# Local and strided attention into a gated mixture of four attentions: wider value products and a fixed order of TensorE's work

## The chip, the cores and the metric

The kernel runs on one core of a Trainium2 chip, in one launch. The metric is the device time of that launch in microseconds. The core has a matrix engine (TensorE, PE in the rows; its weight loads are shown as an engine of their own, PEld), a vector engine (DVE), a scalar engine (ACT), GpSimd (POOL) and SyncE (SP), which issues the transfers here. All five work at once and wait for each other through semaphores. TensorE writes into PSUM, which has eight banks of 128 x 512 floats; the other engines copy from there to SBUF.

## The reference, cut to what matters

```python
# first part: 8 batches, 8 heads, 576 positions, 64 columns a head
rel = pos[:, None] - pos[None, :]
mask_local = (rel >= 0) & (rel < 32)
mask_strided = (rel >= 0) & (pos[None, :] % 32 == pos[:, None] % 32)
# heads 0 to 3 use mask_local, heads 4 to 7 mask_strided
attn = softmax(where(mask, q @ k.T / 8, -1e9))
x = attn @ v                          # heads side by side: 576 x 512 for a batch
# second part: 4 experts, each an attention of 64 columns over x; a token uses its best 2
logits = x @ w_gate
for e in range(4):
    a = softmax(causal(x @ wq[e] @ (x @ wk[e]).T / 8))
    out += weight_of_e_in_the_top_2 * (a @ (x @ wv[e]) @ wo[e])
```

## The kernel before, in words

A batch goes through two stages. **stage1** takes a pair of heads (four pairs a batch: two local, two strided). It loads q and k (`load_qk`, SP), transposes them on TensorE (`tp`, line 875), computes the scores (`s`, line 908), masks them (DVE), runs a softmax in six steps on DVE, POOL and ACT (lines 932 to 943), brings the probabilities the other way round (`tr` on DVE for local heads, `pt` on TensorE at line 972 for strided ones), multiplies with v (`xa`, line 1000 local, line 1019 strided) and splits the result into two numbers of fewer bits, `xh` and `xl`. **The second stage** works on a batch of x: projections (`pj`, lines 1125 and 1136; `vp`, line 1072), scores (`s2`, line 1210; `s2_4`, line 1190), a softmax whose last step is a scaling on POOL (`scale2`, line 1245), transposes (`t2`, line 1264), the product with the values (`acc`, line 1297) and the output matrix (`yp`, line 1326).

A local head looks at 32 positions back, so its 576 queries are 18 blocks of 32, and a block needs the keys of two blocks: the one before and its own. Blocks 0 to 4 stand in partitions 0 to 31, blocks 5 to 9 in the next 32, and so on (`c`, four groups). The product with v at line 1000 takes for every block and each of the two heads two matmuls: 32 partitions, the 64 columns of v as weights, 32 columns of probabilities. These are 35 x 2 = 70 matmuls for a pair of heads, and an f32 matmul runs as two pairs of a weight load and a matmul, so 140 pairs.

TensorE's array is used in **six shapes of tile**, called modes in the code: 128x128 (`pj`, `vp`, `s2_4`, `yp`), 64x128 (`tp`, `pt`, `t2`, `s2`), 128x64 (`acc`), 64x64 (strided `s` and `xa`), 64x32 (local `s`) and 32x64 (local `xa`).

No engine's order is written out by hand. `op(kind, engines, key, function, ...)` records an operation with a modelled duration, and `schedule()` then emits all of them engine by engine: whenever an engine is free in its model it takes, of the operations that could start first, the one with the smallest key. The key is a due time plus a number from a table `PRI` (one row for each kind and batch). For TensorE five is added to the key if the mode would change:

```python
k = o.key + (MODE_PEN if e == "PE" and mode not in (None, o.mode) else 0.0)
...
if t < 26.0:
    d *= 1.5
if mode not in (None, o.mode):
    d += 0.09 + o.first
elif t > free[e] + 0.05:
    d += 0.08
```

On the chip every engine then works through its list in that order and waits in place for what is not ready. What schedule() chooses also decides which of the eight banks (`RB`), which of two buffers of probabilities (`P2`) and which of two input buffers (`NAT`) an operation gets.

Of the kernel before, what the change touches and what calls it, by code (L numbers as in the profile page):

```python
# [14 lines left out]
NEG = -1.0e9  # L15
# [5 lines left out]
def attention_moe_kernel(  # L21
# [26 lines left out]
    STR = 32  # L48
# [15 lines left out]
    class Op:  # L64
        __slots__ = ("eng", "key", "fn", "mode", "npk", "allocs", "uses", "succ", "ndep", "ready", "end", "left", "first")
# [15 lines left out]
    class Ring:  # L81
# [16 lines left out]
        def take(self, buf):  # L98
# [1305 lines left out]
```

## Time and profile before

| what | value |
|---|---|
| median of 3 runs | 522.42 us (514.83 to 523.39) |
| the profiled execution | 523.32 us, its span 521.6 us |
| PE busy | 478.3 us, 92% of the span, 9,126 weight loads and as many matmuls |
| DVE, ACT, POOL busy | 328.4, 288.7 and 201.9 us |
| moved by the DMA queues | 42.05 MB, 81 GB/s over the span |
| mean granted clock of TensorE | 0.930 of full speed |

The table is read from the top: the engine with the largest busy share first, then what share the others have. Busy time of PE is not time at full rate: a matmul of few columns holds the engine for its passage while others run beside it in other tiles, so the prediction measures from start to start.

### The profile page before, as it was taken

To read this page: it belongs to the slowest core of one execution; us is meant where nothing else is said; L and a number is where in the kernel's file an instruction comes from. 1 tells how busy PE (TensorE), PEld (TensorE's weight loads), DVE (VectorE), ACT (ScalarE), POOL (GpSimd) and SP (SyncE) were. 2 spreads that over 40 slices of the span, in tenths; PEclk is the share of its full clock that TensorE was granted. 3 is DMA by queue.
4 is the path that set the end of the run, shared out by engine and by line. 5 is a ranking of instruction groups with operands and counts; after the bars stand their busy time and mean duration, and the time that the engine had idled before them with its cause. 6 is when DMAs were issued, how large, how long until landed. Compare 5 with 4: busy or idle time off the path is not lost.

```text
span 521.6 us, 21771 instructions
## 1 busy us (share of the span) xinstructions
PE 478.3 (92%) x9126; PEld 422.0 (81%) x9126; DVE 328.4 (63%) x1057; ACT 288.7 (55%) x870; POOL 201.9 (39%) x320
## 2 busy tenths in 40 slices
PE   6668989998897999998898999979999799999996
PEld 5557879996676799997777899769987798789874
DVE  4745947567865665776677546768787346863850
ACT  3335647655865434666585435754487226762862
POOL 5443725434722241456145212733265013720440
PEclk9555999999989899999889999989999799999999
DMA  7566571207436432301334620274013400210013
GB/s 144 125 146 139 116 129 35 53 1 136 132 88 143 112 81 55 88 2 30 72 98 120 167 88 1 71 142 106 7 48 110 124 1 25 63 64 0 1 63 101
DMA packets 83777, 42.05 MB, mean 81 GB/s; under 512 B 71904, under 2 KB 75360, under 8 KB 83680
## 3 DMA queue, kind: packets, MB, share of 16 engines
q1 hardware_dynamic: 83680, 40.67, 32.3%
q8 instruction: 72, 1.18, 1.0%
q14 instruction: 25, 0.20, 0.1%
HBM read 31.20 MB, written 9.44 MB: 78 GB/s over the span
## 4 chain that ended last, share of the span: by engine, by line
PE 83%; DMA 6%; issue 5%; SPq 3%; DVE 2%; ACT 0%; ACTq 0%; DVEq 0%
PE bank L1125 17%; PE bank L1072 11%; PE bank L1326 11%; PE bank L1297 9%; PE bank L1210 6%; DMA nat<-in_k_dram 6%; PE bank L1264 5%; PE bank L1000 5%; PE bank L875 4%; PE bank L908 4%; PE bank L1190 3%; PE bank L1136 3%; PE bank L1019 3%; PE bank L972 2%; SPq L822 2%
## 5 line engine op out<-in xcount | busy, mean ns | idle before, releaser
L1245 POOL TENSOR_SCALAR p<-p,st,wt 128x512 f32<-128x512 f32 (+3 forms) x128 | 76.5, 613 | 66.6 <-DVE st L1229 25.5
L1222 ACT ACTIVATE p<-p,st 128x128 f32<-128x128 f32 (+3 forms) x128 | 71.5, 562 | 10.2 <-DVE st L1217 10.1
L1217 DVE CUSTOM_DVE_ANT_0 p<-bank,m_cau 128x256 f32<-128x256 f32 (+3 forms) x128 | 55.6, 486 | 5.1 <-PE bank L1210 4.6
L683 ACT COPY th<-bank 128x384 f32<-128x384 f32 (+2 forms) x117 | 45.7, 434 | 13.8 <-PE bank L1264 12.7
L683 ACT COPY qkt<-bank 128x324 f32<-128x324 f32 (+2 forms) x99 | 36.8, 426 | 29.1 <-PE bank L875 24.8
L1297 PE MATMUL bank<-th,vs 128*64 128x192 f32 (+4 forms) x512 | 52.5, 355 | 0.0
L1145 ACT CAST qk<-bank 128x288 fp32r<-128x288 f32 x64 | 25.5, 398 | 48.2 <-PE bank L1125 43.4
L934 POOL TENSOR_TENSOR p1l<-p1l,st 128x640 f32<-128x640 f32 (+1 forms) x18 | 20.5, 1141 | 73.3 <-DVE st L932 55.5
L986 DVE TENSOR_TENSOR xl<-bank,xh 128x160 fp32r<-128x160 f32 (+4 forms) x112 | 31.3, 327 | 26.8 <-ACT xh L984 26.1
L1297 PEld LDWEIGHTS bank<-th,vs 128*64 128x64 f32 x512 | 35.5, 143 | 14.8 <-issue 8.1
L984 ACT CAST xh<-bank 128x160 fp32r<-128x160 f32 (+4 forms) x112 | 27.3, 322 | 36.4 <-PE bank L1000 30.9
L1147 DVE TENSOR_TENSOR qkl<-bank,qk 128x288 fp32r<-128x288 f32 x64 | 28.7, 452 | 29.0 <-ACT qk L1145 28.7
L875 PE MATMUL bank<-ident,nat 54*128 54x54 f32 (+1 forms) x636 | 35.3, 252 | 12.4 <-DMA nat<-in_k_dram 7.8
L1072 PE MATMUL bank<-wh_v,xh 128*128 128x260 f32 (+1 forms) x160 | 46.2, 289 | 0.1
L1072 PE MATMUL bank<-wl_v,xh 128*128 128x260 f32 (+1 forms) x160 | 46.0, 288 | 0.3 <-DVE wl_v L778 0.3
L1072 PE MATMUL bank<-wh_v,xl 128*128 128x260 f32 (+1 forms) x160 | 46.1, 288 | 0.0
L1000 PE MATMUL bank<-pt,v 32*64 32x32 f32 x2240 | 30.5, 232 | 15.6 <-issue 15.3
L1000 PEld LDWEIGHTS bank<-pt,v 32*64 32x64 f32 x2240 | 27.8, 140 | 18.9 <-issue 17.2
L875 PEld LDWEIGHTS bank<-ident,nat 54*128 54x128 f32 (+1 forms) x636 | 29.5, 162 | 16.6 <-issue 6.5
L1264 PE MATMUL bank<-ident,p 64*128 64x64 f32 x800 | 41.2, 231 | 0.2
L1264 PEld LDWEIGHTS bank<-ident,p 64*128 64x128 f32 x800 | 33.1, 141 | 8.3 <-issue 4.8
L908 PE MATMUL bank<-qkt 64*32 64x64 f32 (+1 forms) x2048 | 35.2, 245 | 2.7 <-issue 1.9
(146 smaller groups left out, 1320.6 us busy)
## 6 DMA issues: line engine op xcount, KB each, us to landing
out_dram<-ys SPq DMA_DIRECT2D x32, 256.0 KB
nat<-in_k_dram SPq DMA_DIRECT2D x28, 144.0 KB
nat<-in_q_dram SPq DMA_DIRECT2D x28, 144.0 KB
nat<-in_q_dram SPq DMA_DIRECT2D x32, 99.0 KB
nat<-in_k_dram SPq DMA_DIRECT2D x32, 99.0 KB
v<-in_v_dram SPq DMA_DIRECT2D x64, 48.0 KB
v<-in_v_dram SPq DMA_DIRECT2D x48, 54.0 KB
nat<-in_q_dram SPq DMA_DIRECT2D x16, 90.0 KB
```

Of the source, the lines that this page charges most:

```text
L683: (nc.scalar.copy if e == "ACT" else nc.vector.tensor_copy)(dst, src)
L875: nc.tensor.transpose(tp[x].t[:, w_ * (g - g0):w_ * (g - g0) + w_], blk, ident[r, r])
L908: nc.tensor.matmul(o, lhs, rhs, start=True, stop=True)
L1000: nc.tensor.matmul(xa[c].t[64 * h:64 * h + 64, 32 * i:32 * i + 32], vv()[r, h, i + own, :], pv2()[r, h, i, 32 * own * (g > 0):32 * own * ( ...
L1072: nc.tensor.matmul(vp.t[:m, :NV], xx.t[:, t0:t0 + m], ww.t[:, kt, :], start=i == 0, stop=i == 11)
L1125: nc.tensor.matmul(pj.t[:, :HS], ww.t[:, kt, ep * 128:(ep + 1) * 128], xx.t[:, c], start=i == 0, stop=i == 11)
L1217: lambda e, sp=sp, p=p, a=a, nk=nk, ci=ci: nc.vector.tensor_tensor_reduce(out=p.t[:, a, :nk], in0=sp[a].t[:, :nk], in1=m_cau[:, S - nk:], ...
L1222: op("exp2", {"ACT": 0.33 + 0.00083 * nk}, k_ + 1, lambda e, p=p, a=a, ci=ci, nk=nk: nc.scalar.activation(p.t[:, a, :nk], p.t[:, a, :nk], ...
L1245: lambda e, p=p, a=a, ci=ci, t=t, nk=nk: nc.gpsimd.tensor_scalar(p.t[:, a, :nk], p.t[:, a, :nk], st.t[:, 14 + ci + a:15 + ci + a], wt.t[:, ...
L1264: nc.tensor.transpose(tp[hf].t[:, 64 * c:64 * c + 64], src, ident[r, r])
L1297: nc.tensor.matmul(acc.t[o, c0:c0 + cn], vw, th[a].t[:, s0:s0 + cn], start=j == 0, stop=j == idx[-1], skip_group_check=True)
L1326: nc.tensor.matmul(yp.t[:, :DM], xx.t[:, c0:c0 + 128], ww.t[:, ep, :], start=i == 0, stop=i == 5)
```

## The change

Three things change, and the table of numbers.

First, at line 1000 (1014 after) a matmul no longer serves one query block. A block of v is the "own" block of one query block and the "block before" of the next, and both stand side by side in the transposed probabilities. So one matmul with 64 columns of probabilities writes both; at the ends of a group of five it has 32. A pair of heads has 21 x 2 = 42 matmuls, 84 pairs. To make that regular, query block 0 has keys before the start of the sequence as its first 32 columns, and the mask sets them to -1e9 with one memset in place of a memset and a POOL selection.

Second, on TensorE `PRI` no longer holds numbers that are added to a due time but the places of the operations in one sequence, 0, 1, 2 and so on; `schedule()` takes them in that order, and waits in its model if the next one is not ready. `MODE_PEN` goes. The other engines keep keys, with new numbers.

Third, the model counts TensorE's instructions (`ni` pairs an operation): they come in parts of 256, a part is asked for 40 instructions before the part ahead of it begins, and it is there 4.0 us later; TensorE waits at its first instruction until then. This is in the model alone; nothing on the chip is changed by it but the order that follows.

```diff
-        o.eng, o.fn, o.mode, o.npk = eng, fn, mode, npk
+        o.eng, o.fn, o.mode, o.npk, o.ni = eng, fn, mode, npk, 2 * ni
...
-        o.key = round(key + PRI[at][SEQ[at]], 3)
+        o.key = PRI[at][SEQ[at]] if "PE" in eng else round(key + PRI[at][SEQ[at]], 3)
...
+    FETCH = 4.0
...
+        turn = 0
+        done, ask, part, here, coming = 0, 193 - 40, 193, 0.0, 0.0
...
+                if e == "PE":
+                    cand = [o for o in cand if o.key == turn]
...
-                        k = o.key + (MODE_PEN if e == "PE" and mode not in (None, o.mode) else 0.0)
+                        k = o.key
...
+                end, rate = t + d, d / o.ni
+                while min(ask, part) <= done + o.ni:
+                    x = min(ask, part)
+                    at = end - (done + o.ni - x) * rate
+                    if x == ask:
+                        coming, ask = at + FETCH, ask + 256
+                    else:
+                        end += max(here - at, 0.0)
+                        here, part = coming, part + 256
+                done += o.ni
+                d = end - t
...
-    nc.vector.memset(m_loc[0:32, 0], 0.0)
-    keep(m_loc[0:32, 0], [[-1, 64]], 0, 1)
+    nc.vector.memset(m_loc[0:32, 0, :STR], NEG)
...
-                            lhs, rhs = qv(0, STR * g, STR)[r], qv(1, max(STR * g - STR, 0), 64)[r]
+                            lhs, rhs = qv(0, STR * g, STR)[r], qv(1, STR * g - STR, 64)[r]
...
-                for i in range(5):
-                    for own in range(2):
-                        for c in range(4):
-                            g = 5 * c + i
-                            if g > 17 or g + own == 0:
-                                continue
-                            r = slice(32 * c, 32 * c + 32)
-                            for h in range(2):
-                                nc.tensor.matmul(xa[c].t[64 * h:64 * h + 64, 32 * i:32 * i + 32], vv()[r, h, i + own, :],
-                                                 pv2()[r, h, i, 32 * own * (g > 0):32 * own * (g > 0) + 32],
-                                                 start=own == 0 or g == 0, stop=own == 1)
-
-            op("xa", {"PE": 1.2}, k0, values1, r=[vt, ptt], w=[*xa, *(x[u] for x in (xh, xl) for u in range(4))], mode=MV)
+                for j in range(6):
+                    for c in range(4):
+                        first, last = int(c == 0), 3 if c == 3 else 5
+                        if not first <= j <= last:
+                            continue
+                        r = slice(32 * c, 32 * c + 32)
+                        c0, c1 = max(j - 1, 0), min(j + 1, last)
+                        p0, p1 = max(64 * j - 32, 0), min(64 * j + 32, 64 * last)
+                        for h in range(2):
+                            nc.tensor.matmul(xa[c].t[64 * h:64 * h + 64, 32 * c0:32 * c1], vv()[r, h, j, :],
+                                             ptt.t[r, 320 * h + p0:320 * h + p1],
+                                             start=j == first, stop=j == last, skip_group_check=True)
+
+            op("xa", {"PE": 0.74}, k0, values1, r=[vt, ptt], w=[*xa, *(x[u] for x in (xh, xl) for u in range(4))], mode=MV, ni=84)
```

What the table does to the order is best seen in the lists of TensorE's instructions. In both fences below, a row is a matmul of the program with the tile it writes, the tiles it reads and the size of its output; x2 is two in a row, and each f32 matmul counts once.

The first place is the local value products, on TensorE. Before, the two of the third batch stand one behind the other between an output tile (line 1326) and an accumulation (line 1297):

```order
L1326 MATMUL bank_67<-wl_o_242,oh_222 128x512
L1000 MATMUL bank_70<-pt_188,v_180 64x32 x2
L1000 MATMUL bank_71<-pt_188,v_180 64x32 x2
L1000 MATMUL bank_69<-pt_188,v_180 64x32 x2
...
L1000 MATMUL bank_66<-pt_187,v_179 64x32 x2
L1000 MATMUL bank_67<-pt_187,v_179 64x32 x2
L1297 MATMUL bank_70<-th_166,vs_207 64x384
```

Now such a product stands alone, here one of the fifth batch behind a strided one (line 1033), with 64 columns in most matmuls:

```order
L1033 MATMUL bank_67<-pt_185,v_177 64x54 x2
L1014 MATMUL bank_66<-pt_184,v_176 64x32 x2
L1014 MATMUL bank_64<-pt_184,v_176 64x32 x2
L1014 MATMUL bank_68<-pt_184,v_176 64x32 x2
L1014 MATMUL bank_69<-pt_184,v_176 64x64 x2
...
L1014 MATMUL bank_64<-pt_184,v_176 64x32 x2
L1311 MATMUL bank_65<-th_162,vs_202 64x384
```

A pair of heads takes 70 rows' worth of matmuls in the one list and 42 in the other. Two local products in a row stood at two places and now stand at one, in the last batch.

The second place shows the modes, on TensorE. Before, an output tile (line 1326, mode 128x128) stands alone between transposes (line 1264, 64x128) and local scores (line 908, 64x32), and the next output tile comes behind those scores:

```order
L1264 MATMUL bank_64<-ident,p_157 128x64
L1326 MATMUL bank_67<-wh_o_241,oh_221 128x512
...
L1326 MATMUL bank_67<-wl_o_242,oh_222 128x512
L908 MATMUL bank_69<-qkt_178 32x64
...
L908 MATMUL bank_70<-qkt_178 32x64
L1326 MATMUL bank_67<-wh_o_241,oh_221 128x512
```

Now, behind local scores (line 921), an output tile (line 1340), scores of the last tile (line 1204) and value projections (line 1086) follow each other, all of mode 128x128:

```order
L921 MATMUL bank_66<-qkt_174 32x64
L1340 MATMUL bank_67<-wh_o_238,oh_220 128x512
...
L1340 MATMUL bank_67<-wl_o_239,oh_218 128x512
L1204 MATMUL bank_69<-qk_140,qd_144 128x288 x2
L1204 MATMUL bank_69<-qkl_143,qd_144 128x288
L1204 MATMUL bank_71<-qk_141,qd_145 128x288 x2
L1204 MATMUL bank_71<-qkl_142,qd_145 128x288
L1086 MATMUL bank_65<-wh_v_236,xh_191 128x260
```

Over the whole list the mode changes 210 times before and 139 times after.

## Rows read from the trace of the kernel before

**Rows 1.** The page: busy time and share by engine; granted clock in 40 slices.

```profile
PE 478.3 (92%) x9126; PEld 422.0 (81%) x9126; DVE 328.4 (63%) x1057; ACT 288.7 (55%) x870; POOL 201.9 (39%) x320
...
PEclk9555999999989899999889999989999799999999
```

**Rows 2.** Two stretches: busy time (x instructions) by engine, clock, DMA share, GB/s.

```profile
0.00:52.40 52.40, 36.26 (x1003) 32.14 (x1004) 28.15 (x88) 20.59 (x59) 22.94 (x45) 0.61 0.64 138
52.40:520.00 467.60, 442.07 (x8125) 389.91 (x8123) 300.26 (x970) 268.07 (x812) 178.96 (x277) 0.97 0.30 74
```

**Rows 3.** PE's waits after 52.4 us: total, times, longest.

```profile
PE bank L1000 <- issue: 12.7, 8, 2.7
PE bank L875 <- DMA nat<-in_k_dram: 3.9, 3, 2.4
PE bank L875 <- DVE st L938: 2.7, 2, 2.1
PE bank L908 <- issue: 1.9, 1, 1.9
```

**Rows 4.** PE's waits before 52.4 us, those on nothing the profile shows.

```profile
PE bank L1000 <- issue: 2.6, 1, 2.6
...
PE bank L972 <- issue: 2.3, 1, 2.3
```

**Rows 5.** The page's DMA queues: packets, MB, share of 16 engines.

```profile
q8 instruction: 72, 1.18, 1.0%
```

**Rows 6.** Timeline of PE, a local value product: start, duration, what [idle before].

```profile
81.33 0.30 PE L1136 MATMUL bank<-xl,wh_q 128*128 128x288 f32 x1
81.47 0.29 PE L1136 MATMUL bank<-xh,wl_q 128*128 128x288 f32 x1
81.69 1.63 PE L1000 MATMUL bank<-pt,v 32*64 32x32 f32 x140
83.25 0.40 PE L1136 MATMUL bank<-xh,wh_k 128*128 128x288 f32 x1
83.49 0.29 PE L1136 MATMUL bank<-xl,wh_k 128*128 128x288 f32 x1
```

**Rows 7.** Timeline of PE at local scores and two value products.

```profile
135.73 0.40 PE L1326 MATMUL bank<-wh_o,ol 128*128 128x512 f32 x1
135.97 0.39 PE L1326 MATMUL bank<-wl_o,oh 128*128 128x512 f32 x1
136.29 1.04 PE L908 MATMUL bank<-qkt 64*32 64x64 f32 x80
137.25 0.50 PE L1326 MATMUL bank<-wh_o,oh 128*128 128x512 f32 x1
137.59 0.39 PE L1326 MATMUL bank<-wh_o,ol 128*128 128x512 f32 x1
...
138.84 1.87 PE L1000 MATMUL bank<-pt,v 32*64 32x32 f32 x164
142.93 1.40 PE L1000 MATMUL bank<-pt,v 32*64 32x32 f32 x116 [2.22 <-issue]
```

**Rows 8.** Timeline of PE at strided scores.

```profile
129.35 0.92 PE L908 MATMUL bank<-qkt 64*64 64x54 f32 x48
130.20 0.46 PE L1264 MATMUL bank<-ident,p 64*128 64x64 f32 x8
```

**Rows 9.** First and last of eight stretches of low clock after 52.4 us.

```profile
76.30:79.70 3.40, 3.40 (x16) 3.40 (x15) 2.21 (x8) 1.50 (x6) 0.00 (x0) 0.50 0.32 92
...
410.80:417.70 6.90, 5.83 (x104) 5.59 (x105) 2.43 (x6) 1.01 (x4) 1.26 (x1) 0.51 0.27 72
```

**Rows 10.** Timeline of PE inside the first of these stretches.

```profile
76.63 0.44 PE L1136 MATMUL bank<-xh,wh_q 128*128 128x288 f32 x1
76.87 0.44 PE L1136 MATMUL bank<-xl,wh_q 128*128 128x288 f32 x1
```

**Rows 11.** The page: copies from PSUM on ACT.

```profile
L683 ACT COPY th<-bank 128x384 f32<-128x384 f32 (+2 forms) x117 | 45.7, 434 | 13.8 <-PE bank L1264 12.7
```

More of the change, by code (lines that the diff above doesn't have):

```diff
@@ L64, in attention_moe_kernel @@
     class Op:
-        __slots__ = ("eng", "key", "fn", "mode", "npk", "allocs", "uses", "succ", "ndep", "ready", "end", "left", "first")
+        __slots__ = ("eng", "key", "fn", "mode", "npk", "allocs", "uses", "succ", "ndep", "ready", "end", "left", "first", "ni")
     class Buf:
@@ L108, in attention_moe_kernel, with op @@
     PRI = {
[421 rows of a table removed]
[420 rows of a table added]
     }
-    def op(kind, eng, key, fn, r=(), w=(), mode=None, npk=0, after=(), first=None):
+    def op(kind, eng, key, fn, r=(), w=(), mode=None, npk=0, after=(), first=None, ni=0):
         o = Op()
-        o.eng, o.fn, o.mode, o.npk = eng, fn, mode, npk
+        o.eng, o.fn, o.mode, o.npk, o.ni = eng, fn, mode, npk, 2 * ni
         o.first = (0.104 if mode == "128x128" else 0.05) if first is None else first
@@ L625, in schedule @@
             if e == "PE":
+                turn += 1
                 if t < 26.0:
@@ L653, in schedule @@
             n += 1
-    MODE_PEN = 5.0
     RB = Ring("bank", [128, 512], F32, 8, pool=pp)
@@ L875, in tps @@
                         nc.tensor.transpose(tp[x].t[:, w_ * (g - g0):w_ * (g - g0) + w_], blk, ident[r, r])
-            op("tp", {"PE": 0.058 * (g1 - g0) + 0.03}, k0 - 14 + u, tps, r=[nat], w=[*tp, qkt], mode=MR)
+            op("tp", {"PE": 0.058 * (g1 - g0) + 0.03}, k0 - 14 + u, tps, r=[nat], w=[*tp, qkt], mode=MR, ni=2 * (g1 - g0))
             for x in range(2):
@@ L908, in scores @@
                         nc.tensor.matmul(o, lhs, rhs, start=True, stop=True)
-        op("s", {"PE": 0.6 if local else 0.75}, k0 - 11, scores, r=[qkt], w=[*sp, p[0], p[1]], mode=ML if local else MQ)
+        op("s", {"PE": 0.6 if local else 0.75}, k0 - 11, scores, r=[qkt], w=[*sp, p[0], p[1]], mode=ML if local else MQ, ni=80 if local else 48)
         N = 2 * ni * nk
@@ L973, in tps2 @@
                                             p.t[r, b_, 2 * m:2 * m + 2].rearrange("p i c -> p (i c)"), ident[r, r])
-            op("pt", {"PE": 0.062 * ni + 0.01}, k0 - 2, tps2, r=[p[0], p[1]], w=[*pt, ptt], mode=MR)
+            op("pt", {"PE": 0.062 * ni + 0.01}, k0 - 2, tps2, r=[p[0], p[1]], w=[*pt, ptt], mode=MR, ni=12)
             for hf in range(2):
@@ L1020, in values1 @@
                                              pv2()[r, h ^ b_, b_, m, :n_], start=True, stop=True)
-            op("xa", {"PE": 0.63}, k0, values1, r=[vt, ptt], w=[*xa, *(x[u] for x in (xh, xl) for u in range(3))], mode=MQ)
+            op("xa", {"PE": 0.63}, k0, values1, r=[vt, ptt], w=[*xa, *(x[u] for x in (xh, xl) for u in range(3))], mode=MQ, ni=44)
             def runs(g0, gn, rn):
@@ L1073, in mm @@
                         i += 1
-            op("vp", {"PE": 12 * 0.12}, key + step * t, mm, r=xbufs(b) + wbufs("v"), w=[vp, vs[t]], mode=M128)
+            op("vp", {"PE": 12 * 0.12}, key + step * t, mm, r=xbufs(b) + wbufs("v"), w=[vp, vs[t]], mode=M128, ni=12)
             op("vp_out", either(NV), key + step * t + 0.5, lambda e, t=t, m=m, vp=vp: copy(e, vs.t[:m, t, :], vp.t[:m, :NV]),
@@ L1140, in project @@
                                r=[X[b, kt][i][x] for i in range(2) for x in range(4)] + [W[nm][i][kt] for i in range(2)],
-                               w=[pj, qk[j, u]], mode=M128, after=prev)]
+                               w=[pj, qk[j, u]], mode=M128, after=prev, ni=3)]
             else:
-                op("pj", {"PE": 12 * 0.1335}, key + step * u, mm, r=xbufs(b) + wbufs(nm), w=[pj, qk[j, u]], mode=M128)
+                op("pj", {"PE": 12 * 0.1335}, key + step * u, mm, r=xbufs(b) + wbufs(nm), w=[pj, qk[j, u]], mode=M128, ni=12)
             c_ = slice(u * HS, (u + 1) * HS)
@@ L1192, in attend @@
                     op("s2_4", {"PE": 0.4}, k_ + 0.2 * hh, mml, r=[qk.d, qk[1, hh], qk.lo[1, hh]],
-                       w=[sp, p[0]], mode=M128)
+                       w=[sp, p[0]], mode=M128, ni=3)
                     op("max2_4", {"DVE": 0.12 + 0.00103 * HS}, k_ + 0.5 + 0.2 * hh,
@@ L1213, in attend @@
                r=[x[0, u] for u in us for x in (qk, qk.lo)] + [x[1, u] for u in range((nk - 1) // HS + 1) for x in (qk, qk.lo)],
-               w=[*sp, p[0], p[1]], mode=MR)
+               w=[*sp, p[0], p[1]], mode=MR, ni=6)
             for a in range(2):
@@ L1267, in attend @@
                           r=[p2[t][0 if a == "l" else a] for t in {t for _, t in blks}], w=[*tp, *(th if a == "l" else [th[a]])],
-                          mode=MR, after=LAST)]
+                          mode=MR, after=LAST, ni=2 * nb)]
             for hf in range(2):
@@ L1302, in attend @@
         op("acc", {"PE": cols * 0.001694 + 0.05}, kk + 4.5, av, r=[vs[j] for j in range(idx[-1] + 1)] + th,
-           w=[acc] + [y[un if i == 0 else b % 2] for i, pair in enumerate(dsts) for y in pair], mode=MC)
+           w=[acc] + [y[un if i == 0 else b % 2] for i, pair in enumerate(dsts) for y in pair], mode=MC, ni=4 * len(range(idx[-1] + 1)))
         parts = [(O[b, ep], un, 384 * un, 64 * un, 384 - 256 * un)]
@@ L1327, in mm @@
                     i += 1
-        op("yp", {"PE": 6 * 0.23}, key, mm, r=need + wbufs("o"), w=[yp, ys], mode=M128)
+        op("yp", {"PE": 6 * 0.23}, key, mm, r=need + wbufs("o"), w=[yp, ys], mode=M128, ni=6)
         op("yp_out", either(DM), key + 0.5, lambda e: copy(e, ys.t, yp.t[:, :DM]), r=[yp], w=[ys])
@@ L1346, in warm @@
             nc.tensor.matmul(wb.t[:, :256], ones[:, :128], ones, start=True, stop=True)
-    op("warm", {"PE": 5.6}, -1e3, warm, w=[wb], mode=M128)
+    op("warm", {"PE": 5.6}, -1e3, warm, w=[wb], mode=M128, ni=14)
     for hp in range(H // 2):
```

841 rows, old and new, of the table PRI are left out of this document.

## The prediction

> **What bounds the kernel now.** I read the page's busy times first, then the waits of the busiest engine, then the timeline where it waits. PE is busy 92% of the span and the next engine, DVE, 63% [rows 1]; behind the start the share is 442.1 of 467.6 us [rows 2]. So the time is what PE needs for its list, plus what it stands still. The reader is to see four things in the rows.
>
> Up to about 52 us loads set the pace: PE is idle for 16 us of 52.4 and its clock is granted at 0.61 on the mean, against 0.97 after that [rows 2].
>
> After that PE waits little for other engines (3.9 us for transfers of k, 2.7 us for a softmax on DVE) but 12.7 + 1.9 = 14.6 us for nothing that the profile shows, 12.7 of it in the middle of local value products [rows 3]; before 52.4 us there are 4.9 us more of the kind [rows 4]. I take these for fetches of PE's own instructions. 18,252 weight loads and matmuls came in 72 packets [rows 1, 5], which is 253 for a packet, and 1.18 MB / 72 is 16 KB: a part of 256 instructions, 128 pairs, that needs a transfer. On the mean a part lasts 522 / 72 = 7.2 us. But from 138.84 us PE ran 164 pairs in under 1.9 us, then stood 2.22 us inside the operation [rows 7]. A request 296 instructions (148 pairs) ahead, which is how the change models it, and some 4 us until arrival fit that.
>
> Such a wait has a second price. After 52.4 us there are eight stretches in which the clock is granted at 0.50, the lower level of 1.2 GHz; seven last 3.4 us and the last one 6.8 [rows 9]. Five of them, the long one included, begin in such a wait or within 2 us behind one: 20.4 us in all. In one, a projection matmul follows the last after 0.24 us [rows 10]; at full clock it is 0.14 [rows 6].
>
> Last, the price of small matmuls goes by their number. A local value product has 140 pairs of 32 columns and takes 83.25 - 81.69 = 1.56 us [rows 6].
>
> **Local value products.** The nearest row to the new form are the local scores: also eight tiles in the array, with 64 columns, 80 pairs in 137.25 - 136.29 = 0.96 us [rows 7]. About 0.15 us of each is the emptying of the array before the next mode, so a pair costs 10.1 ns there and 10.1 ns in the product of 32 columns: twice the columns cost nothing. 84 pairs are then 0.85 + 0.15 = 1.00 us, and 16 products save 16 x 0.56 = 9.0 us. The bounds: the strided scores, with four tiles and 54 columns, need 130.20 - 129.35 = 0.85 us for 48 pairs [rows 8], 14.6 ns each; by that the saving is 16 x 0.18 = 2.9 us. If a matmul of 64 columns cost twice one of 32, 56 of the 84 pairs would, the sum would be 1.56 us again and the saving nothing. I take 9, from the row with the same number of tiles, and keep 0 to 9.
>
> **Changes of mode.** Counted in the two lists they fall from 210 to 139, by 71. The price from rows: output matmuls follow each other after 0.24 us, the first local score after 0.32, so 0.08 on that side [rows 7]; on the way back the first output matmul holds 0.34 in place of 0.24, and 0.15 us of the scores is their tail. That is 0.33 for two changes. I take 0.13 for one, between 0.08, the least that shows on one side, and 0.17: 71 x 0.13 = 9 us, with bounds of 6 and 12.
>
> **Fetches.** Fewer pairs (16 x 56 = 896 of 9,126) are seven parts less, worth nothing by themselves. What counts is how often 148 pairs go by in less than 4 us. I laid durations by kind, taken as in rows 6 to 8, along both lists. Before, 20 of 70 parts come too late, by 25 us in all, where the trace has 20 us of waits; after, 6 of 63 do, four of them in the start, and the two later ones lack 1 us together. So of 14.6 us some 14 go. The bounds are 0, if the waits only move, and 14.6. Here the Trainium skill speaks against the change: Runtime: NRT & Kernel Launch, section "Instruction fetch mechanics", says that an engine's next page is fetched while it executes the current one and that this is mostly hidden. By that sentence the fetch model would buy nothing here and this term would be 0 (the second rival); this trace, with waits of 14.6 us that no engine or transfer ends, disagrees for dense stretches.
>
> **Clock.** If the five waits that precede a drop go, 20.4 us at 0.50 go too. Work like the projections' gains 0.10 of 0.24 us, 42%; transposes and scores in such stretches gain less. I take 0.4 x 20.4 = 8 us, bounds 0 (with the waits) and 9.
>
> **The start.** Two local products and waits of 4.9 us lie in it, at half clock. Some of it is hidden by the loads, which run at 138 GB/s there [rows 2] and in nearly the same order after, and the dense parts left are in the start. I take 2 us, bounds 0 and 5.
>
> **What may come in their place.** PE's sequence is one fixed list in either kernel once it runs, so a later wait is possible wherever the new list is closer to its supplier. I compared the PE work that stands between supplier and user, in the same durations. Between the last scores of a unit and its first transposes the least is 7.0 us before and 8.3 after; between x of a batch and its first projection 2.1 and 2.5; between an input buffer's last use and its next, behind the start, 6.3 and (once) 5.5. Only the transposes of the last tile come closer, 10.8 before and 7.4 at the very end after. The chains as a whole get no tighter. The banks do: a bank taken again after under 1 us of PE work is seen 42 times before and 68 after, since more of one kind stands together. A copy out of a bank takes 0.43 us [rows 11]; I charge half of one, 0.2 us, for 26 more places: 5 us lost, with bounds of 0 and 20 (68 places at 0.3).
> The mask's memset in place of a memset and a POOL selection is at the start, behind other selections and ahead of data that arrive later: nothing. If that cover failed it would be below 1 us. The new numbers of the other engines' keys I cost at nothing beyond these distances; DVE would be busy 328 of some 485 us, 68%, which leaves it off the bound.
>
> **Sum.** -9 - 9 - 14 - 8 - 2 + 5 = -37. Against the profiled execution, 523.3 us, that is 486; that execution lies 0.9 us above the median of 522.4, which the measured change will be set against. I say 486.
>
> **The rivals.**
> - *Value products dearer than their neighbours.* A weight load and 64 columns in the same row group could stand in each other's way, which the local scores, with 32 columns of weights, don't show. Then the first term is 0 and the time 495. For it: no row has that form. Against it: the 32-column form with the same weights is as fast per pair as the scores.
> - *Fetch waits stay.* They may be something else than fetches, or fetches that take longer than the model's 4.0 us. Then 14 and 8 are not saved, and the time is 486 + 22 = 508. For it: the profile names no releaser. Against it: the waits stand in the densest code, 12.7 of 14.6 us in local products [rows 3]. The page of the Trainium skill named above (Runtime: NRT & Kernel Launch) is on this rival's side.
> - *New waits on data.* Banks at 20 us in place of 5, each long one followed by a stretch at half clock worth 1.4 us: some eight of these bring 11 us. 486 + 15 + 11 = 512, and 10 more of the same makes "no change".
> - *Slower.* Transposes (t2) wait in place for POOL's scale2, at the head of each of 32 units. PE takes nothing else meanwhile, as it follows its list. A wait of 1.2 us with a drop of clock worth 1.4 behind it costs 32 x 2.6 = 83 us, and the time is 569. It decides from 1.5 us a unit, wait and drop together (48 us): above that the kernel is slower than 533. For it: a unit's chain over DVE, ACT and POOL is the longest. Against it: the 8.3 us above, no wait of this kind in the trace, and POOL at 39%.
>
> **How the numbers follow.** A measurement of this kernel can tell a change from none at about 2%, 10 us: faster is under 512, slower over 533. My forecast has 0.58, with its own range of 474 to 498 (the terms at 12 + 9 + 14.6 + 9 + 5 with no new waits would give 474; the lesser price of modes and ten more of waits give about 498). Dear value products have 0.09, fetch waits that stay 0.15, new waits on data 0.12 (half of it above 512), slower 0.06. For 8 in 10 the range takes in the forecast, the first rival and the second up to 510: 472 to 510. Faster has 0.58 + 0.09 + 0.13 + 0.06 = 0.86, slower 0.06 and the same 0.08.
>
> **What would show it.** In the profile after: a local value product of 84 pairs about 1.0 us from start to start (1.4 or more: the first rival). PE's waits on nothing shown after the start near 1 us in place of 14.6, and 65 packets of instructions. Stretches at 0.50 after the start: three or four in place of eight, and a mean granted clock of about 0.95. PE busy near 445 us. Waits on copies or on data above 20 us after the start would make the forecast wrong, and so would a start that ends later than 52 us.

## The result and the profile after

| | before | after |
|---|---|---|
| median | 520.33 us (4 runs, 514.83 to 523.39) | 486.79 us (4 runs, 483.59 to 491.95) |
| ratio | | 0.937, 95% interval 0.921 to 0.953 |
| the profiled execution | 523.32 us, span 521.6 | 491.95 us, span 490.2 |
| TensorE's pairs | 9,126 | 8,230 |
| mean granted clock | 0.930 | 0.950 |

Both profiled executions are the longest of their kernels' runs and are left out of the ratio; the two traces are compared with each other: 31.4 us of span.

The page of the changed kernel: busy time by engine, and the queue of TensorE's instructions. They are to be held against [rows 1, 5].

```profile
PE 452.1 (92%) x8230; PEld 407.4 (83%) x8230; DVE 331.9 (68%) x1065; ACT 285.6 (58%) x862; POOL 201.0 (41%) x319
...
q8 instruction: 65, 1.06, 0.9%
```

PE is still 92% busy, so it still sets the time. The packets fall by seven. In two stretches, as in [rows 2] (the long stretch at a low clock now ends at 41.5 us and not at 52.4):

```profile
0.00:41.50 41.50, 27.36 (x722) 23.05 (x723) 23.17 (x77) 15.61 (x43) 19.72 (x41) 0.67 0.71 142
41.50:488.00 446.50, 424.79 (x7513) 384.37 (x7507) 308.70 (x988) 269.98 (x820) 181.25 (x279) 0.98 0.33 80
```

PE's waits after 41.5 us (what waited, for what: total, times, longest), to be held against [rows 3]:

```profile
PE bank L921 <- issue: 7.9, 5, 3.0
PE bank L888 <- DMA nat<-in_q_dram: 6.3, 3, 3.1
PE bank L888 <- DMA nat<-in_k_dram: 3.4, 2, 1.9
PE bank L888 <- ACT xh L997: 1.3, 1, 1.3
PE bank L1014 <- issue: 0.8, 1, 0.8
```

The waits that nothing in the profile ends ("issue") have not gone: 7.9 + 0.8 = 8.7 us stand against 14.6. They have moved from the value products to the local scores. Loads of q and k now hold PE for 9.7 us; before it was 3.9 us, for k alone. A softmax no longer does.

The timeline of PE at a local value product, as in [rows 6], and at the longest of the waits (start, duration, what, [idle before it]):

```profile
112.51 1.11 PE L1014 MATMUL bank<-pt,v 32*64 32x32 f32 x84
113.56 1.30 PE L1311 MATMUL bank<-th,vs 128*64 128x384 f32 x8
...
232.32 1.67 PE L921 MATMUL bank<-qkt 64*32 64x64 f32 x137
237.03 0.65 PE L921 MATMUL bank<-qkt 64*32 64x64 f32 x23 [3.04 <-issue]
```

The product takes 113.56 - 112.51 = 1.05 us for its 84 pairs. The wait stands inside one operation of 160 pairs, behind the 137th.

**Where the time went.** The table divides the spans. For every step of PE, from the start of one matmul to the start of the next, I took the usual time of its kind at full clock. "Work" is the sum of these usual times. "Modes" is what the steps with a change of mode take above them, "low clock" what the steps in stretches at 0.50 take above them, and waits are steps with PE idle over 0.15 us. With another choice of the usual time a column moves by 1 to 4 us and a difference by up to 2.

| us of the span | work | modes (changes) | low clock | waits on nothing shown | waits on data | the two ends |
|---|---|---|---|---|---|---|
| before | 427.9 | 24.1 (210) | 26.5 | 20.1 | 16.4 | 6.6 |
| after | 417.6 | 16.8 (139) | 17.8 | 10.1 | 22.5 | 5.5 |
| difference | -10.3 | -7.3 | -8.7 | -10.0 | +6.1 | -1.1 |

### The profile page after: what moved, and what is told of

The parts are those of the page before. It is cut to its first block, busy times and chain, and to the rows that moved or that the text cites. A ratio compares the mean times of both kernels' runs of the same rounds, so it can differ in the third digit from the quotient of the medians.

```text
span 490.2 us, 19979 instructions
## 1 busy us (share of the span) xinstructions
PE 452.1 (92%) x8230; PEld 407.4 (83%) x8230; DVE 331.9 (68%) x1065; ACT 285.6 (58%) x862; POOL 201.0 (41%) x319
## 4 chain that ended last, share of the span: by engine, by line
PE 81%; DMA 8%; SPq 6%; issue 3%; ACT 1%; DVE 1%; POOL 0%; ACTq 0%
PE bank L1139 18%; PE bank L1340 11%; PE bank L1086 10%; PE bank L1311 8%; PE bank L1224 7%; PE bank L1278 6%; PE bank L921 5%; PE bank L888 4%; DMA nat<-in_k_dram 4%; DMA nat<-in_q_dram 3%; PE bank L1014 3%; PE bank L1204 3%; PE bank L1033 3%; SPq L865 3%; SPq L835 2%
## 5 line engine op out<-in xcount | busy, mean ns | idle before, releaser
L1259 POOL TENSOR_SCALAR p<-p,st,wt 128x256 f32<-128x256 f32 (+3 forms) x128 | 76.4, 613 | 68.8 <-DVE st L1243 37.6
L1236 ACT ACTIVATE p<-p,st 128x256 f32<-128x256 f32 (+3 forms) x128 | 71.8, 571 | 1.5 <-DVE st L1231 1.4
L1231 DVE CUSTOM_DVE_ANT_0 p<-bank,m_cau 128x384 f32<-128x384 f32 (+3 forms) x128 | 57.5, 485 | 3.6 <-PE bank L1224 2.4
L697 ACT COPY th<-bank 128x256 f32<-128x256 f32 (+2 forms) x122 | 46.9, 434 | 7.0 <-PE bank L1278 6.5
L888 PE MATMUL bank<-ident,nat 54*128 54x54 f32 (+1 forms) x636 | 33.8, 241 | 16.4 <-DMA nat<-in_k_dram 7.3
L1311 PE MATMUL bank<-th,vs 128*64 128x192 f32 (+4 forms) x512 | 48.8, 340 | 0.0
L697 ACT COPY qkt<-bank 128x324 f32<-128x324 f32 (+2 forms) x82 | 31.1, 423 | 26.4 <-PE bank L888 26.0
L888 PEld LDWEIGHTS bank<-ident,nat 54*128 54x128 f32 (+1 forms) x636 | 28.8, 152 | 20.1 <-issue 15.0
L947 POOL TENSOR_TENSOR p1s<-p1s,st 128x648 f32<-128x648 f32 (+1 forms) x18 | 20.9, 1167 | 48.5 <-DVE st L945 48.5
L921 PEld LDWEIGHTS bank<-qkt 64*32 64x32 f32 (+1 forms) x2048 | 29.2, 126 | 13.4 <-issue 9.2
L1278 PEld LDWEIGHTS bank<-ident,p 64*128 64x128 f32 x800 | 35.3, 142 | 4.1 <-issue 1.4
L697 DVE COPY qkt<-bank 128x324 f32<-128x324 f32 (+2 forms) x46 | 21.0, 473 | 23.6 <-PE bank L888 23.3
```

What stands on the lines that cost most here:

```text
L697: (nc.scalar.copy if e == "ACT" else nc.vector.tensor_copy)(dst, src)
L888: nc.tensor.transpose(tp[x].t[:, w_ * (g - g0):w_ * (g - g0) + w_], blk, ident[r, r])
L921: nc.tensor.matmul(o, lhs, rhs, start=True, stop=True)
L947: nc.gpsimd.tensor_tensor(P, P, bc[0], ALU.subtract)
L1231: lambda e, sp=sp, p=p, a=a, nk=nk, ci=ci: nc.vector.tensor_tensor_reduce(out=p.t[:, a, :nk], in0=sp[a].t[:, :nk], in1=m_cau[:, S - nk:], ...
L1236: op("exp2", {"ACT": 0.33 + 0.00083 * nk}, k_ + 1, lambda e, p=p, a=a, ci=ci, nk=nk: nc.scalar.activation(p.t[:, a, :nk], p.t[:, a, :nk], ...
```

## The experiments

The question is not whether the kernel is faster but which part of it earned what, why waits on nothing shown are left, and why loads now hold PE. Theory: these waits are fetches of TensorE's instructions, and the loads stand next behind them. Rivals: the waits are something else (banks, a semaphore), or the order alone is the gain.

**One part alone (e1, e2).** e1 is the kernel after with the value loop of the kernel before; its first query block reads the masked half of its probabilities, so that block's values come out as zero.

```diff
-                for j in range(6):
-                    for c in range(4):
...
+                for i in range(5):
+                    for own in range(2):
+                        for c in range(4):
...
```

> The changed kernel, with only the local value products as before (70 matmuls of 32 columns for a pair of heads). Theory: a product takes 1.56 us again in place of 1.05, so 16 x 0.51 = 8 us more of matmuls, and denser parts of instructions add some 3 to 8 us of fetch waits, so 498 to 504 us against 487. Rival (the fixed sequence alone makes the gain, and wider products only shift time into waits): within 3 us of 487.

Measured: 506.99 us (503.42 to 513.93), ratio 0.978 [0.972, 0.985]; the interval reaches across 2%, so whether the order alone is worth that much is not settled. It is slower than I expected, and PE's waits from 60 to 470 us say why:

```profile
PE bank L1013 <- issue: 9.1, 5, 2.5
PE bank L921 <- issue: 3.2, 2, 2.5
PE bank L1277 <- issue: 1.9, 1, 1.9
PE bank L1085 <- issue: 1.1, 1, 1.1
```

With thick products the new order still waits 15.3 us on nothing shown, the kernel before 14.6 [rows 3]. Changes of mode cost 16.2 us, as in the kernel after. So this order earned the modes, and no fetches. It was laid for 84 pairs a product, though, so with 140 its borders fall elsewhere than its model has them; what an order laid for thick products would save is not shown.

e2 is the kernel before with the new value loop and mask alone; the order comes from the old table.

```diff
-    nc.vector.memset(m_loc[0:32, 0], 0.0)
-    keep(m_loc[0:32, 0], [[-1, 64]], 0, 1)
+    nc.vector.memset(m_loc[0:32, 0, :STR], NEG)
...
-                for i in range(5):
...
+                for j in range(6):
...
```

> The kernel before, in its own order, with only the wider local value products (42 matmuls). Theory: 8 us less of matmuls, and less dense parts: the fetch waits after the start, 14.6 us, fall to some 8, with fewer stretches at half clock: 500 to 506 us against 520. Rival (a product's matmuls count alone, fetch waits stay): 511 to 513.

Measured: 499.26 us (498.08 to 500.80), ratio 0.966 [0.960, 0.971], a little below the range expected. PE's waits from 52 to 497 us:

```profile
PE bank L907 <- issue: 4.2, 3, 2.2
PE bank L874 <- DMA nat<-in_k_dram: 3.7, 4, 1.8
PE bank L1000 <- DMA v<-in_v_dram: 2.4, 2, 1.4
...
PE bank L1000 <- issue: 0.9, 1, 0.9
```

Here the waits on nothing shown have fallen, to 5.1 us in these rows (5.7 with three smaller ones), without the new order and without its model of fetches. The excess at low clock is 16.5 us, against 23.9 in e1: it fell along with these waits. Against the 517.35 us of the kernel before in the same comparison, the order alone gives 10.4 us and the products alone 18.1; together 28.5, of a difference that is 27.8 to 33.5 us in the two comparisons of the whole change.

**Where the waits stand.** If they are fetches of parts of 256 instructions, they must end at fixed places in the list. The model in the code counts a weight load and a matmul for each pair. But the trace also has PE's semaphore instructions, 206 of them before and 216 after. Counting the instructions ahead of the first matmul behind a wait, with and without these (the column of semaphores has one more, a drain at the start of the list):

| trace | time, us | pairs x 2 | semaphores | sum |
|---|---|---|---|---|
| before | 75.33 | 2,710 | 43 | 10 x 256 + 193 |
| before | 245.90 | 9,294 | 115 | 36 x 256 + 193 |
| before | 411.87 | 15,626 | 183 | 61 x 256 + 193 |
| after | 88.52 | 3,202 | 63 | 12 x 256 + 193 |
| after | 237.03 | 8,762 | 135 | 34 x 256 + 193 |
| after | 356.71 | 13,070 | 179 | 51 x 256 + 193 |

The sum is always 192 or 193 above a multiple of 256, in every such wait of over 0.25 us of either trace. Semaphores were what the model lacked: its border lies 63 instructions off at 88 us and 179 at 357, where a dense operation of 160 pairs has 320. The window up to the longest wait of after shows the pairs (4,382 matmuls of PE, the last being the one that waited):

```profile
0.00:237.03 237.03, 209.32 (x4382) 190.73 (x4382) 170.24 (x532) 135.94 (x408) 107.11 (x169) 0.93 0.48 104
```

The trace also keeps the start and the end of each transfer of instructions on the queue q8, one for each part. Of these waits there are 10 before and 7 after, and each ends 1.2 to 1.7 us behind the end of such a transfer, every time the one whose number is that of the border: the wait at 34 x 256 + 193 ends at 237.03 us, 1.57 us behind the 34th transfer, which ran from 234.09 to 235.46 us. So these waits are fetches. The earliest transfers start 290 to 300 instructions ahead of their borders, which fits a request some 296 ahead.

**The borders shifted (e3, e4).** A theory of fetches says that instructions put in front of everything move the waits. e3 adds 25 tiny matmuls, 100 instructions, to the warm-up of the kernel after, e4 38, 152 instructions. The order of all else stays.

```diff
+        for i in range(25):
+            o = slice(32 * (i % 4), 32 * (i % 4) + 32)
+            nc.tensor.matmul(wb.t[o, 256:264], ones[:64, :32], ones[:64, :8], start=True, stop=True)
```

> The changed kernel with 100 more TensorE instructions (25 tiny matmuls) behind the warm-up, which shift every later border between parts of 256 instructions by 100 and nothing else. Theory (the waits on nothing shown are fetches and end at the first instruction of a part, all of TensorE's instructions counted): the waits at the scores near 237 and 356 us are gone, the one near 88 us stays, small ones come near 138, 250 and 315 us; in sum 3 to 6 us after the start in place of 8.4, total 482 to 487. Rival (they belong to the operations, data or banks): waits at the same scores as before, sum unchanged.

> The same with 152 more instructions (38 tiny matmuls). Theory: waits near 88 us and new ones of 2 to 3 us near 312 and 357 and 1 to 2 us near 408 us, none near 237; in sum 7 to 11 us after the start, total 485 to 492. Rival: as in the run with 100, the same places as without any.

Measured, e3: 486.49 us (485.37 to 486.75), ratio 0.940 [0.936, 0.945]. Its timeline at the three operations that waited in the kernel after:

```profile
88.09 0.79 PE L921 MATMUL bank<-qkt 64*32 64x64 f32 x56 [1.67 <-issue]
...
235.87 2.17 PE L921 MATMUL bank<-qkt 64*32 64x64 f32 x160
...
350.16 1.82 PE L921 MATMUL bank<-qkt 64*32 64x64 f32 x160
```

The two later ones run through their 160 pairs; the first waits at another pair, again at 12 x 256 + 193. Of the small waits expected near 138, 250 and 315 us only the first came. The waits of e3 from 60 to 470 us, and behind them the longest group of the kernel after in the same stretch:

```profile
PE bank L888 <- DMA v<-in_v_dram: 4.3, 1, 4.3
PE bank L888 <- DMA nat<-in_q_dram: 2.9, 2, 2.2
PE bank L888 <- DMA nat<-in_k_dram: 2.7, 2, 1.4
PE bank L921 <- issue: 1.7, 1, 1.7
...
PE bank L1033 <- issue: 0.9, 1, 0.9
```

```profile
PE bank L921 <- issue: 6.8, 3, 3.0
```

Waits on nothing shown fell from 6.8 + 0.8 = 7.6 to 2.6 us. Waits on loads are as long as before, 9.9 us against 9.7, so they did not take what came free. Whether the time fell is not settled, as no kernel without the padding was timed beside e3: its 0.940 stands between 0.937 and 0.946 (e9, below) for the unchanged kernel. Its profiled execution spans 484.9 us, 4.2 less than that of e9.

Measured, e4: 491.60 us (487.99 to 494.31), ratio 0.950 [0.944, 0.957], 5.1 us above e3 in the same comparison. Three waits in its timeline:

```profile
86.48 1.28 PE L921 MATMUL bank<-qkt 64*64 64x54 f32 x82 [0.86 <-issue]
...
305.94 0.32 PE L921 MATMUL bank<-qkt 64*32 64x64 f32 x10 [2.30 <-issue]
...
352.43 0.31 PE L921 MATMUL bank<-qkt 64*32 64x64 f32 x7 [1.98 <-issue]
```

They came back where the count put them, at 45 x 256 + 192 and 52 x 256 + 193 for the last two; their sum behind the start, 5.4 us, is less than the 7 to 11 expected. The wait belongs to the place in the list and not to the operation: this settles the rival of banks and semaphores.

**The price of a change of mode (e5, e6).** Each of 40 value projections gets a tiny matmul in its middle, of another mode in e5 (two changes more) and of its own in e6.

```diff
+                        if i == 6:
+                            nc.tensor.matmul(vp.t[0:64, 400:432], ident[0:32, :64], ident[0:32, :32],
+                                             start=False, stop=True, skip_group_check=True)
```

In e6 the operands are `vp.t[:, 400:432], ident, ident[:, :32]`.

> The changed kernel with one tiny matmul (32 rows, 64 columns of weights, 32 columns, f32, so two pairs) of mode 32x64 in the middle of each of the 40 value projections (line 1086), which adds 80 changes of mode. It is read against the next run, which has as many instructions. Theory (a change costs about 0.13 us): the way from the projection matmul ahead of it to the one behind it is 0.26 us longer than there, less the difference of the two tiny pairs, at full clock. Rival (a change costs under 0.05 us in the stream of work, and the shape of the order matters for other reasons): less than 0.1 us longer.

> Control for the run before: the same number of tiny matmuls (32 columns, f32) in the mode of the projection itself, 128x128, no change of mode. Expected about 0.12 us for the two pairs on top of the 0.12 us between neighbours.

Measured: 504.57 us for e5 and 498.68 for e6, one run each. The difference of 5.9 us for 80 changes is 0.07 each, with the spread of single runs on it. The timelines, e5 first, are the better measure:

```profile
160.74 0.28 PE L1089 MATMUL bank<-wl_v,xh 128*128 128x260 f32 x1
160.95 0.30 PE L1087 MATMUL bank<-ident 32*64 32x32 f32 x2
161.18 0.39 PE L1089 MATMUL bank<-wh_v,xh 128*128 128x260 f32 x1
161.40 0.28 PE L1089 MATMUL bank<-wh_v,xl 128*128 128x260 f32 x1
```

```profile
162.24 0.29 PE L1089 MATMUL bank<-wl_v,xh 128*128 128x260 f32 x1
162.36 0.30 PE L1087 MATMUL bank<-ident 128*128 128x32 f32 x2
162.50 0.37 PE L1089 MATMUL bank<-wh_v,xh 128*128 128x260 f32 x1
162.70 0.28 PE L1089 MATMUL bank<-wh_v,xl 128*128 128x260 f32 x1
```

The same four starts take 0.66 us with two changes and 0.46 without, and so do the medians of the 39 projections at full clock: 0.10 us a change, if the two tiny pairs cost the same in either mode. The table above has 7.3 us for 71 changes, 0.10 as well.

**What the loads cost (e7).** The kernel after, whose third to eighth batches load no q, k or v and compute on what the buffers hold.

```diff
+            if b > 1:
+                return
```

> The changed kernel without the loads of q, k and v for batches 3 to 8 (their work runs on what the buffers hold, so the output is wrong for them). Theory 1 (after the change TensorE waits for late loads of q and k, and a fetch of instructions takes longer when the DMA engines carry data): the 11 us of waits on loads after the start are gone, waits at the first instruction of a part shrink from 8.7 us to 3 to 6, at the same places, stretches at half clock nearly go: 465 to 472 us. Theory 2 (a fetch always takes about 4 us): the same waits on fetches as before the edit, 8 us, total 470 to 475. Rival (the waits at the transposes of q and k come from another engine): total within 3 us of 487.

Measured: 471.83 us (469.80 to 473.28), ratio 0.918 [0.910, 0.926]. The stretch behind the start, and PE's waits in it:

```profile
53.40:471.00 417.60, 409.05 (x7344) 371.39 (x7340) 303.12 (x974) 265.42 (x809) 177.08 (x274) 0.99 0.09 30
```

```profile
PE bank L925 <- issue: 2.8, 2, 1.7
PE bank L1344 <- issue: 1.2, 1, 1.2
PE bank L1315 <- issue: 0.9, 1, 0.9
```

So the loads cost the kernel after some 10 to 15 us: 0.918 stands against 0.937 and, in e9, 0.946. Waits on nothing shown are there without them too, 4.9 us. How much of the fall from 8.7 us is the loads' doing e7 does not tell: its list has 111 semaphore instructions in place of 216, so the borders meet other pairs (34 x 256 + 192 lies in an output tile, line 1344).

Where loads run, a part can come later. From the start of the instruction 296 ahead of the border to the end of the wait, e7 shows 3.6 to 3.9 us four times behind the start. Of the twelve such waits of over half a microsecond in the traces of before and after, four take 3.4 to 4.0 us, three 4.3 to 4.6 and five 5.2 to 7.1. In these twelve the transfer itself takes 0.9 to 1.4 us, and PE goes on 1.2 to 1.6 us behind its end. What differs is its start: 1.0 to 1.7 us behind that instruction in the four short cases, 2.3 to 4.7 in the five long ones, and 0.9 to 1.3 in e7.

**Why a load is late.** SyncE's list in the kernel after (start of issue, duration, what):

```profile
137.97 9.53 SPq L865 DMA_DIRECT2D v<-in_v_dram  x16
147.60 1.02 SPq L842 DMA_DIRECT2D nat<-in_q_dram  x3
148.72 1.00 SPq L842 DMA_DIRECT2D nat<-in_k_dram  x3
```

Sixteen transfers of v take SyncE 9.53 us and stand ahead of q and k, which PE waits for from 149.6 us on. The first of them starts 2.4 us after SyncE got to it, when a value product on PE (line 1014) has freed the buffer of v. The model charges 1.4 us for four such transfers, 5.6 us for the sixteen.

**More room for the loads (e8, e10, e11, with e9 as the mark).** e8 has a third input buffer and the 100 instructions of e3. e10 has the third buffer, and puts the first batch's v ahead of the extra loads of q and k. e11 is e10 with the 100 instructions. e9 is the kernel after, unchanged, beside e10 and e11.

```diff
-    NAT = fixed("nat", [128, (11 * 2 + 1) * D], 2, ...
+    NAT = fixed("nat", [128, (11 * 2 + 1) * D], 3, ...
...
-            op("load_v", {"SP": 1.4 if local else 2.6}, (k0 - 25 if b else 4.0 + hp), ...
+            op("load_v", {"SP": 1.4 if local else 2.6}, (k0 - 25 if b else hp - 396.0), ...
```

> The changed kernel with the 100 padding instructions of e3 and a third buffer for the loads of q and k (NAT), which lets them be issued earlier; the order of TensorE stays, the model orders the other engines anew. Theory (loads late by their place in SP's list take what the fetches gave): waits on loads of q and k after the start fall from 13 us to below 5, total 474 to 481. Rival (the loads are late because the DMA engines are full): no change, 484 to 488.

> The changed kernel itself, timed beside the two that follow on the same chip: 483 to 490 us.

> The changed kernel with a third buffer for the loads of q and k and with the loads of v for the first batch moved ahead of those of q and k for the second (in e8 TensorE stood 10.2 us for v in the start). No padding. Theory: waits on loads after the start stay below 5 us as in e8, the start is no longer than in the changed kernel, fetch waits are its own 8 to 10 us: 474 to 480. Rival (e8's gain came from the padding alone): 484 to 488.

> The same with the 100 padding instructions of e3. Theory: the fetch waits after the start fall to some 3 us as in e3 and e8, and with early loads this is not given back: 470 to 476 us, 3 to 6 below the run without padding. Rival (padding is worth nothing, as in e3): equal to the run without it.

| kernel | median, us (runs) | ratio to before |
|---|---|---|
| e8 | 478.74 (476.67 to 480.18) | 0.933 [0.925, 0.940] |
| e9 | 490.47 (484.00 to 493.29) | 0.946 [0.940, 0.952] |
| e10 | 480.59 (479.20 to 482.42) | 0.930 [0.925, 0.934] |
| e11 | 475.14 (473.84 to 475.77) | 0.919 [0.914, 0.923] |

e8 and e11 lie in their ranges, e9 and e10 0.5 and 0.6 us above theirs. In e8 no wait on q or k is left from 60 to 470 us, so they had been late by the list of SyncE and its buffers; the rival, DMA engines that are full, fails.

e8's waits in its first 40 us show the cost of the third buffer there:

```profile
PE bank L1014 <- DMA v<-in_v_dram: 10.2, 1, 10.2
PE bank L921 <- issue: 4.5, 1, 4.5
```

SyncE loaded q and k ahead and v behind them; hence the key in e10. Waits from 60 to 470 us, e9, then e10, then e11:

```profile
PE bank L888 <- DMA nat<-in_q_dram: 7.8, 3, 3.2
PE bank L921 <- issue: 6.3, 3, 3.0
PE bank L888 <- DMA nat<-in_k_dram: 2.2, 2, 1.9
```

```profile
PE bank L921 <- issue: 4.6, 4, 2.2
PE bank L1014 <- issue: 2.0, 2, 1.2
```

```profile
PE bank L921 <- issue: 1.3, 2, 1.2
PE bank L1033 <- issue: 0.7, 1, 0.7
PE bank L1014 <- issue: 0.5, 1, 0.5
```

In e9 loads hold PE for 7.8 + 2.2 us, in e10 no such wait is left in this stretch; the medians are 9.9 us apart. The fetch waits are worth their time: from e10 to e11 they fall by 4.1 us, the excess at low clock by 1 to 2, and the median by 5.5. I had taken e3 to say that late loads hide this gain; its rows do not show that. e11 is the best version here, 12 to 15 us below the two medians of the kernel after.

## Why the prediction was right, step by step

The time came out at 486.79 us for 486 forecast, but one term came to less than half. That the two are within 1 us is luck: the errors of the terms go both ways, and the median lies 5 us below the profiled execution, 491.95 us, which is what the sum against 523.3 us speaks of.

- **Local value products, -9.** Right: 1.05 us where 1.00 was forecast and 1.56 was measured before, so 16 x 0.51 = 8.2 us. The row of local scores, with as many tiles, was the right one to take; the first rival's twofold price did not show.
- **Changes of mode, -9.** The count of 71 was right, the price of 0.13 too high: 0.10 by e5 and e6, so -7.3.
- **Fetches, -14 after the start.** This term failed in size and in reason. It measured -6, from 14.6 to 8.7. I laid the durations along the lists with the borders of the kernel's model, which leaves out the semaphore instructions, and with 4.0 us for each part, where some took 7. e1 shows that this order saved no fetches, e2 that the fall comes with the products, which have 56 pairs fewer each. Fewer pairs, which I called worth nothing by themselves, also make the dense stretches shorter, and that counted. The second rival was right that the waits would stay with the order alone; of its two causes the first is wrong, as they are fetches, and the second holds for the five that took 5.2 us or more. The Trainium skill (Runtime: NRT & Kernel Launch, section "Instruction fetch mechanics") calls fetching mostly hidden; the traces disagree, with 20.1 us of waits before and 10.1 after.
- **Clock, -8.** It measured -8.7, but over the whole span, and the term was for the time behind the start. There the stretches at 0.50 fell from 30.8 us to 20.4, by 10.4 where I had let 20.4 go, which is some 5 us of the 8.7; the rest lies in the start. Four stretches lie behind the start of the kernel after, three or four were forecast. But their cause has changed: one begins in the fetch wait of 237.03 us (the row below, read as in [rows 2]), and ahead of the others, at 72.3, 154.2 and 260.0 us, PE had waited for q or k. The wait of 2.37 us that ends at 356.71 us has no such stretch behind it.

```profile
236.10:242.90 6.80, 5.87 (x38) 4.93 (x39) 3.40 (x9) 1.68 (x5) 1.26 (x1) 0.50 0.27 44
```

- **The start, -2.** Mis-sized. Its low clock ended 11 us earlier, at 41.5 us, which is worth some 4 us; waits on nothing shown in it fell from 5.4 to 1.4 us, and waits on data grew by 2: some -6 in all.
- **What may come in their place, +5.** Right in size, wrong in place, so the size is luck. Waits on data grew by 6.1 us, 4.3 of them behind the start, but on loads of q and k and not on banks. I had measured the work between an input buffer's last use and its next on PE's side, where it looked nearly as wide as before, and not the list of SyncE, in which 16 transfers of v stand ahead.
- **Waits for scale2.** No such wait shows; t2 (line 1278) waits for nothing in these rows. The slower rival did not come up.

The sum of the table is -31.3, of the prediction -37. Behind the start the fetches lack 8 us and the clock 3, and the modes lack 2; the start brought 4 more than forecast, the ends 1, and the work column 2 more than the products account for, whose cause stays open. The mean clock is 0.95 and the packets 65, as forecast; PE busy is 452 and not 445 us.

What stays open: why the transfer of a part starts 1 us behind its request at some places and over 4 at others. Loads run in the long cases, and e7 has none of these, but it leaves out the loads of all later batches at once and does not tell which transfer stands in the way.

## What to carry to other kernels

When the busiest engine stands still and nothing in the profile ends the wait, count all its instructions up to that place, its semaphores too: if waits end at equal places modulo 256, thinner dense operations help, and instructions put in front move the borders. A gain of a few microseconds needs the kernel without it in the same comparison, as e10 stands beside e11; in e3, without one, it could not be told. A queue's own list, with the measured time of each issue, belongs in the estimate as much as the list of the engine that sets the time.

## What the hardware showed that I had not expected

A hundred tiny instructions ahead of all the work made the kernel faster by 5.5 us (e10 to e11), since they shifted which pair meets a border. From the instruction 296 ahead, a part takes 3.6 to 3.9 us even where no q, k or v is loaded (e7): where 148 pairs run faster than that in these traces, as in local scores and products, PE waits if a border falls behind them. And PE's semaphore instructions, which the profile doesn't count as busy, count for these borders.
